# Maxima's rows on SP's queue 14 slots behind a block's input, four extra maxima rounds in output units, score heads together amid projections

## The chip, the cores and the metric

The kernel runs on one core of a Trainium2 chip. The metric is the device time of one execution in microseconds, the median of three runs: 2252.01 us (2251.91 to 2252.19). Five engines work side by side, each through its own queue in order: TensorE (PE; its weight loads are shown as PEld), VectorE (DVE), ScalarE (ACT), GpSimd (POOL) and SyncE (SP), which here only issues DMAs. DMAs are issued by SP and, a few, by ACT.

## The reference

One sequence of 2048 tokens with 576 features goes through attention with 32 heads of 18 features, and through an MLP with 4608 hidden features behind a layer norm; a gate for each token mixes the two.

```python
def reference(A_x, A_wqkv, A_wo, B_x, B_w1, B_b1, B_w2, B_b2, gate_w):
    x = A_x
    g = _sigmoid((x * gate_w).sum(-1, keepdims=True))
    a = _A_ref(x, A_wqkv, A_wo)          # softmax(q k^T / sqrt(18)) v, then wo
    b = _B_ref(x, B_w1, B_b1, B_w2, B_b2)  # gelu(layernorm(x) w1 + b1) w2 + b2
    return g * a + (1 - g) * b
```

## The kernel before, in words

Matmuls run in a rounded 32-bit format; where precision matters an operand is split into a high and a low part, and three products are summed. A first stage (to about 237 us) makes Q, K, V and the normed tokens and writes them to DRAM. Then comes one long loop, in which attention and MLP are woven into each other, and at the end the output projection.

**Attention.** A unit is a pair of heads and half of the queries; there are 32 units of 16 key blocks, so 512 steps. The softmax's maximum is taken in a first pass: `s1_round` (L216) computes for a query tile and 512 keys the scores of both heads (matmul L227, one head on rows 0 to 53 of the array, the other on rows 64 to 117), and VectorE reduces them (L229). A unit has 32 such rounds. When a unit's rounds are done, `s1_finish` (L232) turns the maxima into two rows for each head, which are stored into rows 54 and 55 of the unit's Q tile `qa` with eight small DMAs from the tile `mr` (L257, issued in helper line L134; these are "the rows" below), so that the second pass `s2` (L299) gets scores that are shifted by the maximum already: score matmul L310 on 56 rows, then the exponential on ScalarE (L312) into a ring of tiles. `pv` (L327) multiplies them with V (L338) for several steps at once.

In a step of the loop, `s2` runs twice: head 0's score, a round of a later unit between, head 1's score. Where there is no round, head 1's score (`tail`) is held back (`held`) until the next `flush()`, and other PE work stands between the two heads. Score tiles of the first pass rotate over three PSUM banks, those of the second over two.

**MLP.** Tokens come in 4 blocks of 512, hidden features in 9 groups of 4 chunks. For each group, `h_pair` (L554) computes two chunks of hidden features (matmul L581, input `Y`, weights W1), then a GELU chain on ACT, POOL and DVE; `out_pair` (L677) is the output unit: one tile of 128 tokens, 24 pairs of matmuls (L713, weights W2) in two turns, with a lent round between the turns (`lend_round`), and two sums on DVE (L687). The W2 tiles of a group are four (`w3` in the program, 4 buffers), so the next group's can be loaded only when the last output unit of this group has read them. In the first block they are split on ACT and POOL from raw weights (L475, L480); later they are reloaded from `w_scr` (one DMA of 576 KB each, L134). At a change of the token block, `load_y` (L738) loads the next block's input while the last `h_pair` of the old block still runs; its DMAs stand in SP's queue and wait for parts of the old input to be read.

**Order and queues.** All is written out by hand: generators yield pieces of MLP work, `fill` (L1339) puts them between a step's parts, and `run_due` counts slots; work put off with `defer(n, ...)` runs n slots later. The framework keeps each engine's order and adds the semaphores. Each DMA counts on one of eight completion semaphores, handed out in turn in the order in which the framework lists the instructions, and is issued only when the DMA before it on the same semaphore has landed. The rows go out on SP at once, in a bundle, unless `slot[0] < ybusy[0]`: then they go out on ScalarE's queue, one in each of the next eight slots. `load_y` sets `ybusy` to 30 slots ahead each time it is called, so that the rows don't stand on SP behind the input.

**Four rounds more.** The loop takes two rounds in each step. So that the rounds end earlier, four are taken ahead of the loop, and four more (`extra`, `LEAD = 4`) at the first four PV products of the loop (L1391), by `next_round`, a round with both heads in a row.

**The end.** When MLP work is used up (after about 2165 us), `fill` takes matmuls of the output projection (`out_proj`, L1300, on all 128 rows) to put between the scores, eight in each gap. Behind the last PV, the denominators of the last unit go through DRAM (L351 to L368) and are loaded for the last blocks (L1201); ACT and DVE prepare the blocks (L1227 to L1239), PE does what is left of the projections.

Of the kernel before, what the change touches and what calls it, by code (L numbers as in the profile page):

```python
# [29 lines left out]
G = 4  # L30
# [10 lines left out]
LEAD = 4  # L41
# [19 lines left out]
def gated_mix_kernel(ctx: ExitStack, tc: tile.TileContext, x, wqkv, wo, w1, b1, w2, b2, gate_w, out):  # L61
# [58 lines left out]
    def psum(pool):  # L120
        return pool.tile([P, TB], F32, name="ps")

    def big_tile():
        return yp.tile([P, 9, TB], F32R, name="big")
# [12 lines left out]
    slot = [0]  # L137
    later = []

    def defer(n, fn):  # L140
        later.append((slot[0] + n, fn))
# [128 lines left out]
    ybusy = [0]  # L270
# [4 lines left out]
    def flush():  # L275

        if held:
            for fn in waiting:
                fn()
            waiting.clear()  # L280
            tail = held.pop()
            tail()
# [94 lines left out]
    def take_round():  # L377
        u, r = rounds.pop()
        head = s1_round(u, r)
        if r == NR - 1:  # L380
            defer(1, lambda: s1_finish(u))
        return head

    def next_round():
        if rounds:
            flush()
            head = take_round()
            for h in range(2):
                head(h)


    lent = [0]

    def lend_round():
        if rounds and not lent[0]:
            next_round()
            lent[0] = 1
# [7 lines left out]
    def mlp():  # L405
# [90 lines left out]
        def ready(table, key):  # L496
            while key not in table:
                bg.pop(0)[1]()
            return table[key]
# [35 lines left out]
        def cuts(n, pieces):  # L535

            return {(k * n + pieces - 1) // pieces for k in range(1, pieces)}
# [3 lines left out]
        def free_pool():  # L541

            if rounds:
                return ps_w
            turns[0] += 1
            return (ps_s1, ps_w)[(turns[0] - 1) // 2 % 2]
# [130 lines left out]
        def out_pair(i, t, acc):  # L677

            tb, g = seq[i]
            tok = slice(t * P, (t + 1) * P)  # L680
            cs = [slice(nn * ND, (nn + 1) * ND) for nn in range(2)]
            bare = not rounds

            def add(ps, base):
                for nn in range(2):
                    dst = acc[:, t, cs[nn]]
                    nc.vector.scalar_tensor_tensor(dst, ps[nn][:, :ND], 0.5, b2b[:, cs[nn]] if base else dst,  # L687
                                                   op0=ALU.mult, op1=ALU.add)
            ps = [psum(free_pool()) for _ in range(2)]
            ends = {7, 15} if piece[0] == 0 else cuts(24, max(1, 3 - piece[0]))  # L690
            k = 0
            for turn in range(2):
                if turn == 1:
                    flush()
                if turn == 1 and bare:
                    add(ps, g == 0)
                    ps = [psum(free_pool()) for _ in range(2)]
                elif turn == 1:
                    if 3 * G not in ends:
                        lend_round()  # L700
                    turned[0] += 2
                    nc.tensor.wait_ge(turn_sem, turned[0])
                for j in ORDER:
                    while (i, j) not in HT:
                        cut[0] = 3
                        yield 0
                    hh, hl = HT[i, j]
                    w_ = ready(W2, (i * (G // 2) + j // 2, j % 2))
                    for h_, p_ in ((hh, 0), (hh, 1), (hl, 0)):
                        def head(h, h_=h_, p_=p_, w_=w_, k=k, turn=turn, ps=ps):  # L710
                            r = slice(64 * h, 64 * h + 64)
                            nn = h ^ turn
                            mm = nc.tensor.matmul(ps[nn][:, :ND], h_[r, tok], w_[p_][r, cs[nn]],  # L713
                                                  start=(k == 0 or bare and k == 3 * G), stop=(k == 6 * G - 1 or bare and k == 3 * G - 1))
                            if bare:
                                return
                            if k == 3 * G - 1:
                                mm.then_inc(turn_sem, 1)
                                tc.no_tile_sem_insts.add(mm.ins.name)
                                tc.add_to_no_dep_group(f"turn{turned[0]}", mm.ins)  # L720
                            elif k == 3 * G and h == 0:
                                tc.declare_fence(mm.ins, group=f"turn{turned[0] - 2}")
                        weave((0, 1) if turn == 0 else (1, 0), [partial(head, 0), partial(head, 1)], 2)
                        k += 1
                        if k < 6 * G:
                            if k in ends:
                                cut[0] = 1
                            yield 131
            flush()
            add(ps, g == 0 and not bare)  # L730
            if g == NG - 1:
                tt = TBS[tb] * 4 + t
                nc.gpsimd.tensor_scalar(acc[:, t, :], acc[:, t, :], gate1[:, tt:tt + 1], 1.0, op0=ALU.mult, op1=ALU.mult)
                defer(12 if tb < NB - 1 else 4, lambda: nc.sync.dma_start(b_scr[tt * P:(tt + 1) * P, :], acc[:, t, :]))
            cut[0] = 2
            yield 131

        def load_y(tb, s_, c0=0, c1=9):  # L738
            if s_ not in Y:
                Y[s_] = big_tile()  # L740
            ybusy[0] = slot[0] + 30
            for h in range(2):
                dma_r(nc.sync, Y[s_][64 * h:64 * h + 64, c0:c1, :], y_scr[TBS[tb], s_, c0 + h:c1 + h].rearrange("c p n -> p c n"))

# [84 lines left out]
    def filler(upto):  # L829

        while stream and spent[0] < upto:
            try:
                spent[0] += next(stream[0])
            except StopIteration:
                stream.pop(0)
            end, cut[0] = cut[0], 0
            if end == 3:
                break
        run_due()
# [499 lines left out]
    def fill(step):  # L1339

        t = spent[0]
        gap = gaps[0]
        gaps[0] += 1
        if over[0] is None and stream:
            behind[0] = base + (TOTAL - KEPT - base) * step / BARE
            ended[0] = atom() == 2
            piece[0] += 1
            run_due(max(spent[0] - t, GAP))
        if over[0] is None and not stream:
            stream.append(proj)  # L1350
            over[0] = gap - (spent[0] == t)
            spent[0] = 0.0
        if over[0] is not None and over[0] < gap:
            filler(PROJ * 122.5 * (gap - over[0]))
            run_due()

    looped[0] = True
    done = [0]
    due_v = []
    extra = [LEAD]  # L1360
    gaps = [0]
    for u in range(NU):
        for kc in range(NT):
            step = u * NT + kc
            if kc == 1:
                if u + 2 < NU:
                    load_q(u + 2)
                if u % 2 == 0 and u // 2 + 1 < NPAIR - 1:
                    load_k(u // 2 + 1)
                    due_v.append((u * NT, u // 2 + 1))  # L1370
                elif u == NU - 5:
                    ring_stack.close()
                    kp = ctx.enter_context(tc.tile_pool(name="c_ka", bufs=1, side="right"))
                    KA.append(kp.tile([P, S], F32R, name="ka2"))
                    for j in range(2):
                        nc.gpsimd.memset(KA[2][64 * j + 32:64 * j + 64, :].bitcast(F32), 1.0)
                    load_k(NPAIR - 1)
                elif u == NU - 4:
                    due_v.append((u * NT, NPAIR - 1))
            at[0] = step  # L1380

            room[0] = 3 if step < NARROW - 3 else 2
            while due_v and due_v[0][0] <= done[0]:
                load_v(due_v.pop(0)[1])
            s2(u, kc, 0, loop_round(), 462.0)
            if step - done[0] >= room[0] or room[0] == 3 and ended[0] and step > done[0]:
                pv(done[0], step)
                done[0] = step
                piece[0] = 0
                ended[0] = 0  # L1390
                if extra[0]:  # L1391
                    next_round()
                    extra[0] -= 1
            else:
                fill(step)
            s2(u, kc, 1, loop_round(), 462.0)
            if not (room[0] == 3 and ended[0]):
                fill(step)
# [29 lines left out]
```

## Time and profile before

| | |
|---|---|
| median of 3 runs | 2252.01 us |
| the profiled execution itself | 2253.85 us |
| its span in the profile | 2252.1 us |
| mean granted PE clock | 0.997 |
| chain that ended last, share of PE | 95% |
| first stage, loop, projections behind the last PV | to 237, to 2201, to 2249 us |

Times in the profile are microseconds from the start of the span. A row of the timeline gives the start and the length of a group of instructions, engine and line, output <- input, and in brackets the idle time just before it with what ended it. The chain of waits is followed back from the last instruction: what held the end at each moment. Releasers are inferred from semaphores. The granted clock is the share of full speed that PE was allowed. PE's matmuls are pipelined, so neighbours overlap in the timeline.

### The profile page before, as it was taken

Reading aid. Unit: us, or ns where it says so; the run is one execution under the profiler, and the core shown is the slowest. Engines: PE = TensorE matmul, PEld = TensorE weight load, DVE = VectorE, ACT = ScalarE, POOL = GpSimd, SP = SyncE. Lnnn points to the kernel's source line nnn. Section 1 sums busy time; section 2 is a strip of 40 time slices with the busy share of each in tenths; the row PEclk is TensorE's granted clock in tenths of the full one; section 3 lists DMA queues with packets and bytes.
Section 4 is the critical chain, followed back from the end, with each engine's and each line's share of the span. In section 5 each row is a group of like instructions: output and inputs, shape, how many; then the busy total and the mean of one; then the engine's idle time right before and its main releaser. Section 6 shows DMA issues by size and latency. Waiting matters only on the chain.

```text
span 2252.1 us, 51151 instructions
## 1 busy us (share of the span) xinstructions
PE 2228.8 (99%) x20569; PEld 1619.0 (72%) x20569; DVE 1651.6 (73%) x2887; ACT 1440.2 (64%) x2719; POOL 947.0 (42%) x936
## 2 busy tenths in 40 slices
PE   8999999999999999999989999999999999999999
PEld 7878677777677767767667677776676677777768
DVE  5675777777777777777767777777777777777734
ACT  4223677777766666666656666666766667666761
POOL 4002466666654444444435444444534444433420
PEclk9999999999999999999999999999999999999999
DMA  7765654546375434332363424233554333333255
GB/s 243 262 189 183 188 170 146 161 139 191 141 212 183 123 108 132 99 121 99 115 159 141 122 99 122 99 123 120 140 178 114 135 111 103 111 105 113 97 183 169
DMA packets 163411, 323.62 MB, mean 144 GB/s; under 512 B 59838, under 2 KB 86370, under 8 KB 152338
## 3 DMA queue, kind: packets, MB, share of 16 engines
q1 hardware_dynamic: 159174, 313.57, 43.9%
q10 hardware_dynamic: 4000, 6.78, 0.8%
q8 instruction: 162, 2.65, 0.5%
q14 instruction: 75, 0.61, 0.1%
HBM read 229.07 MB, written 95.16 MB: 144 GB/s over the span
## 4 chain that ended last, share of the span: by engine, by line
PE 95%; DVE 2%; DMA 2%; POOL 1%; ACT 1%; issue 0%; SPq 0%; ACTq 0%; DVEq 0%; POOLq 0%
PE ps L338 20%; PE ps L713 20%; PE ps L581 20%; PE ps L310 14%; PE ps L227 11%; PE ps L990 5%; PE ps L1008 2%; PE ps L1300 1%; PE ps L905 1%; DVE m L229 0%; PE ps L1039 0%; DMA x<-in_A_x_dram 0%; DMA w<-w_scr 0%; DMA qa<-mr 0%; DMA ot_scr<-dn_scr 0%
## 5 line engine op out<-in xcount | busy, mean ns | idle before, releaser
L229 DVE TENSOR_REDUCE m<-ps 128x1 f32<-128x512 f32 x2048 | 1302.3, 684 | 333.5 <-PE ps L227 306.5
L312 ACT ACTIVATE p<-ps 128x512 f32<-128x512 f32 x1080 | 587.0, 596 | 294.3 <-PE ps L227 198.9
L310 PE MATMUL ps<-qa,ka 56*128 56x512 f32 x2048 | 704.7, 411 | 3.2 <-DMA qa<-mr 2.1
L312 ACT ACTIVATE ring<-ps 128x512 f32<-128x512 f32 x968 | 525.8, 596 | 282.0 <-PE ps L227 210.4
L227 PE MATMUL ps<-ka,qa 54*128 54x512 f32 x2048 | 648.8, 416 | 3.3 <-DVE m L229 2.2
L713 PE MATMUL ps<-w,hh 64*128 64x288 f32 x4352 | 530.6, 297 | 1.0 <-ACT z L606 0.6
L581 PE MATMUL ps<-big,w 64*128 64x512 f32 x3888 | 516.9, 392 | 0.1
L310 PEld LDWEIGHTS ps<-qa,ka 56*128 56x128 f32 x2048 | 362.4, 185 | 212.0 <-issue 70.1
L180 POOL TENSOR_SCALAR zz<-zz 128x512 f32<-128x512 f32 x272 | 168.2, 619 | 760.5 <-ACT zz L669 728.1
L581 PEld LDWEIGHTS ps<-big,w 64*128 64x128 f32 x3888 | 378.1, 185 | 76.4 <-ACT vt L1019 0.3
L713 PEld LDWEIGHTS ps<-w,hh 64*128 64x128 f32 x4352 | 420.1, 186 | 15.0 <-ACT z L606 1.0
L180 POOL TENSOR_TENSOR zz<-zz,z 128x512 f32<-128x512 f32 x280 | 361.3, 1290 | 36.6 <-ACT zz L671 10.5
L227 PEld LDWEIGHTS ps<-ka,qa 54*128 54x128 f32 x2048 | 339.0, 186 | 36.0 <-DVE m L229 11.8
L713 PE MATMUL ps<-w,hl 64*128 64x288 f32 x2176 | 361.6, 292 | 0.0
L338 PE MATMUL ps<-p,vt 128*32 128x512 f32 x2160 | 265.2, 598 | 0.0
L713 PEld LDWEIGHTS ps<-w,hl 64*128 64x128 f32 x2176 | 247.8, 186 | 1.2
L338 PE MATMUL ps<-ring,vt 128*32 128x512 f32 x1936 | 238.3, 598 | 0.0
L180 POOL TENSOR_TENSOR w<-x,w 128x576 fp32r<-128x576 f32 (+1 forms) x34 | 68.3, 2012 | 276.9 <-ACT w L475 253.8
L180 POOL TENSOR_TENSOR hl<-zz,hh 128x512 fp32r<-128x512 f32 x134 | 174.2, 1300 | 14.5 <-ACT hh L632 3.7
L687 DVE SCALAR_TENSOR_TENSOR x<-ps,x 128x288 f32<-128x288 f32 x268 | 110.2, 453 | 86.9 <-PE ps L713 78.1
L338 PEld LDWEIGHTS ps<-p,vt 128*32 128x32 f32 x2160 | 57.9, 109 | 126.9 <-issue 125.7
L338 PEld LDWEIGHTS ps<-ring,vt 128*32 128x32 f32 x1936 | 52.1, 109 | 112.8 <-issue 112.8
(120 smaller groups left out, 1471.6 us busy)
## 6 DMA issues: line engine op xcount, KB each, us to landing
w<-w_scr SPq DMA_DIRECT2D x54, 1152.0 KB
w<-w_scr SPq DMA_DIRECT2D x108, 576.0 KB
w_scr<-w SPq DMA_DIRECT2D x18, 1152.0 KB
w_scr<-w SPq DMA_DIRECT2D x36, 576.0 KB
qa<-qk_scr SPq DMA_DIRECT2D x192, 72.0 KB
ka<-qk_scr SPq DMA_DIRECT2D x90, 144.0 KB
big<-y_scr SPq DMA_DIRECT2D x48, 256.0 KB
x<-in_B_w_dram SPq DMA_DIRECT2D x34, 288.0 KB
```

The lines of the kernel that those rows point to most:

```text
L180: fn(*args, **kw)
L227: nc.tensor.matmul(ps, qa[r0:r0 + 54, t * P:(t + 1) * P], ka[r0:r0 + 54, kb * TB:(kb + 1) * TB], start=True, stop=True)
L229: nc.vector.tensor_reduce(M4[u][:, h, t, kb:kb + 1], ps, axis=AX.X, op=ALU.max)
L310: nc.tensor.matmul(ps, ka[r0:r0 + 56, kc * P:(kc + 1) * P], qa[r0:r0 + 56, qb * TB:(qb + 1) * TB], start=True, stop=True)
L312: nc.scalar.activation(ring(n)[:, qb, h], ps, AF.Exp, scale=SCALE)
L338: nc.tensor.matmul(OB[u][r:r + 32, :], v[:, k, 19 * h:19 * h + 32], ring(c)[:, qb, h, :], start=(k == 0), stop=(k == NT - 1))
L581: nc.tensor.matmul(ps[h], wt[w_][r, c, :], Y[s_][r, c, :], start=(k == 0), stop=(k == 26))
L687: nc.vector.scalar_tensor_tensor(dst, ps[nn][:, :ND], 0.5, b2b[:, cs[nn]] if base else dst, op0=ALU.mult, op1=ALU.add)
L713: mm = nc.tensor.matmul(ps[nn][:, :ND], h_[r, tok], w_[p_][r, cs[nn]], start=(k == 0 or bare and k == 3 * G), stop=(k == 6 * G - 1 or bare ...
L905: nc.tensor.transpose(ps[:, t * P:(t + 1) * P], x_view(tb)[:, t, c * P:(c + 1) * P], ident)
L990: nc.tensor.matmul(ps, w_[:, c, ms], big[:, s_, :], start=(k == 0), stop=(k == len(prods) - 1))
L1008: nc.tensor.matmul(ps[:, :ND], big[:, s_, tok], w_[:, c, cs], start=(k == 0), stop=False)
```

## The change

Three edits. The rows go to ScalarE's queue only up to 14 slots behind a call of `load_y`, not 30. The four extra rounds aren't taken at the first PV products any more, but within the first four output units, in the second turn, when 20 of the 24 pairs are out. And when `fill` puts projections into a gap, the held score of head 1 is let out first.

```diff
@@ -390,6 +390,7 @@
 
     lent = [0]
+    extra = [LEAD]
 
     def lend_round():
...
@@ -722,6 +723,9 @@
                         weave((0, 1) if turn == 0 else (1, 0), [partial(head, 0), partial(head, 1)], 2)
                         k += 1
+                        if k == 5 * G and extra[0]:
+                            extra[0] -= 1
+                            next_round()
                         if k < 6 * G:
...
@@ -738,7 +742,7 @@
                 Y[s_] = big_tile()
-            ybusy[0] = slot[0] + 30
+            ybusy[0] = slot[0] + 14
...
@@ -1351,13 +1355,13 @@
         if over[0] is not None and over[0] < gap:
+            flush()
             filler(PROJ * 122.5 * (gap - over[0]))
             run_due()
...
-    extra = [LEAD]
     gaps = [0]
...
@@ -1388,9 +1392,6 @@
                 ended[0] = 0
-                if extra[0]:
-                    next_round()
-                    extra[0] -= 1
             else:
```

What moves is little, and each of it in one place. Of 32 units two had their rows on ACT, at the first and at the second change of the input block (about 671 and 1158 us). Around the second one SP's queue stood so before (`w3` are the four W2 reloads, `w4` a W1 reload, `big` the input `Y`):

```order
L134 DMA big_1868<-y_scr_66 64x2x512 x2
L134 DMA big_1306<-y_scr_66 64x2x512 x2
L368 DMA ot_scr_67<-dn_scr_68 36x1x1024
L134 DMA w3_16554<-w2_scr_65 128x1152
L134 DMA w3_16556<-w2_scr_65 128x1152
L134 DMA w3_16558<-w2_scr_65 128x1152
L134 DMA w3_16560<-w2_scr_65 128x1152
L134 DMA w4_16732<-w1_scr_64 128x2304
L353 DMA dn_16840<-oe_16839 128x1x16
```

and ACT's, with the rows between the exponentials (L312):

```order
L134 DMA qa0_109<-mr_16626 2x8x32 x2
L312 ACTIVATE p_2674<-ps_16653 128x512
L312 ACTIVATE p_2674<-ps_16662 128x512
L134 DMA qa0_109<-mr_16626 2x8x32
L606 ACTIVATE z_16676<-ps_16562,b1t_77 128x512
L134 DMA qa0_109<-mr_16626 2x8x32
L312 ACTIVATE ring2_2271<-ps_16687 128x512
L312 ACTIVATE ring2_2271<-ps_16696 128x512
L134 DMA qa0_109<-mr_16626 2x8x32
```

Now ACT has none of them, and SP has all eight between the four W2 reloads and the W1 reload:

```order
L134 DMA w3_16554<-w2_scr_65 128x1152
L134 DMA w3_16556<-w2_scr_65 128x1152
L134 DMA w3_16558<-w2_scr_65 128x1152
L134 DMA w3_16560<-w2_scr_65 128x1152
L134 DMA qa0_109<-mr_16626 2x8x32 x8
L134 DMA w4_16733<-w1_scr_64 128x2304
L353 DMA dn_16840<-oe_16839 128x1x16
```

In the framework's list of all engines, the rows on ACT stood ahead of the W2 reloads on SP and were given their semaphores first; now they come behind them. Around the first change the eight rows stand on SP behind the last input load and ahead of the four stores L480.

The extra rounds, on PE, at the end of one of the first output units (the last L713 here belong to the next unit), before:

```order
L310 MATMUL ps<-qa_109,ka_112 128x512
L227 MATMUL ps<-ka_112,qa_110 128x512 x2
L310 MATMUL ps<-qa_109,ka_112 128x512
L338 MATMUL ps<-ring_2271,vt_114 32x512 x4
L338 MATMUL ps<-ring_2279,vt_114 32x512 x4
L227 MATMUL ps<-ka_112,qa_110 128x512 x2
L310 MATMUL ps<-qa_109,ka_112 128x512
L227 MATMUL ps<-ka_112,qa_110 128x512 x2
L310 MATMUL ps<-qa_109,ka_112 128x512
L713 MATMUL ps<-w_2054,hh 128x288 x4
```

and now, from within the unit:

```order
L714 MATMUL ps<-w_2101,hh 128x288 x4
L227 MATMUL ps<-ka_112,qa_110 128x512 x2
L714 MATMUL ps<-w_2101,hl 128x288 x2
L714 MATMUL ps<-w_2082,hh 128x288 x4
L714 MATMUL ps<-w_2082,hl 128x288 x2
L310 MATMUL ps<-qa_109,ka_112 128x512
L227 MATMUL ps<-ka_112,qa_110 128x512 x2
L310 MATMUL ps<-qa_109,ka_112 128x512
L338 MATMUL ps<-ring_2271,vt_114 32x512 x4
L338 MATMUL ps<-ring_2279,vt_114 32x512 x4
L310 MATMUL ps<-qa_109,ka_112 128x512
L227 MATMUL ps<-ka_112,qa_110 128x512 x2
```

The extra round stood directly ahead of the loop's round; between the two are now eight output matmuls, a round and the PV products. This is so in four units. On DVE the two reductions of the round come ahead of the unit's sums L687.

The scores amid projections, on PE from the first L1300 on, before:

```order
L310 MATMUL ps<-qa_110,ka_28066 128x512 x2
L1300 MATMUL ps<-big 128x288 x8
L310 MATMUL ps<-qa_110,ka_28066 128x512
L1300 MATMUL ps<-big 128x288
L310 MATMUL ps<-qa_110,ka_28066 128x512
L1300 MATMUL ps<-big 128x288
L1300 MATMUL ps<-wlast,big 128x288
L1300 MATMUL ps<-big 128x288 x2
```

and now (L1300 is L1304 there):

```order
L310 MATMUL ps<-qa_110,ka_28066 128x512 x2
L1304 MATMUL ps<-big 128x288 x8
L310 MATMUL ps<-qa_110,ka_28066 128x512 x2
L1304 MATMUL ps<-big 128x288 x2
L1304 MATMUL ps<-wlast,big 128x288
L1304 MATMUL ps<-big 128x288 x2
```

One or two projection matmuls stood between the heads at eight places up to the last PV products; now none do. On ACT the exponential of head 1 moves ahead of some of the block preparations (L1230) that `filler` lets run.

## The prediction

> **What bounds the kernel now.** I read the page's table of engines first, then the list of what TensorE waited for.
>
> ```profile
> PE 2228.8 (99%) x20569; PEld 1619.0 (72%) x20569; DVE 1651.6 (73%) x2887; ACT 1440.2 (64%) x2719; POOL 947.0 (42%) x936
> ```
>
> TensorE (PE) is busy for 2228.8 of 2252.1 us, and no other engine is above three quarters. The instructions on PE are the same in both kernels, 18523 of them in either order, so a gain can come only from the 23.3 us in which PE stands, from time in which it runs at a lower clock, or from neighbours in its queue that overlap better. The list of PE's waits names what stands (engine, line, releaser: us in total, times, longest):
>
> ```profile
> PE ps L713 <- DMA w<-w_scr: 6.1, 2, 5.8
> PE ps L227 <- DVE m L229: 2.2, 4, 0.5
> ```
>
> The first row is, but for 0.3 us, one stall in the middle of the program; the second is four short ones near its start. (PE also waits for the first load, which the change doesn't touch.) I then read the timeline of the stall, PE first (start, us, instructions, in brackets the idle time before them and its releaser), and for comparison the same stretch one group of the MLP earlier.
>
> ```profile
> 1135.06 1.92 PE L338 MATMUL ps<-p,vt 128*32 128x512 f32 x16
> 1143.20 1.06 PE L338 MATMUL ps<-ring,vt 128*32 128x512 f32 x8
> ...
> 1161.64 1.07 PE L338 MATMUL ps<-ring,vt 128*32 128x512 f32 x8
> 1164.93 0.43 PE L713 MATMUL ps<-w,hh 64*128 64x288 f32 x4
> ...
> 1172.26 0.60 PE L713 MATMUL ps<-w,w 64*128 64x288 f32 x2 [5.80 <-DMA w<-w_scr]
> 1178.52 1.92 PE L338 MATMUL ps<-ring,vt 128*32 128x512 f32 x16
> ```
>
> From the start of three steps of PV products, over an output unit, to the next PV products PE takes 1143.20 - 1135.06 = 8.14 us in a normal group, and 1178.52 - 1161.64 = 16.88 us here. So this place costs **8.74 us**, although the wait itself is 5.80. The windows (length, busy time of PE, PEld, DVE, ACT and POOL, granted PE clock, DMA share, GB/s) show the rest:
>
> ```profile
> 1150.00:1160.00 10.00, 10.00 (x88) 6.91 (x86) 7.78 (x16) 5.85 (x13) 0.00 (x0) 1.00 0.03 10
> 1170.00:1175.00 5.00, 2.74 (x18) 2.46 (x20) 1.29 (x2) 1.60 (x3) 0.00 (x0) 0.55 0.47 190
> 1175.00:1180.00 5.00, 5.00 (x48) 3.56 (x46) 3.14 (x6) 2.69 (x5) 0.92 (x2) 0.77 0.00 0
> ```
>
> After the stall the granted clock is 0.55 and then 0.77; the 2.9 us beyond the wait are lost there. The page "TensorE: Matmul & The Clock Gate" of the Trainium skill (section "The HAM clock gate") says that an idle window of about 3.4 us halves PE's clock until it has been busy for about as long. An estimate from that page is 1.7 us lost behind the stall and a sum smaller by 1.2 us; the trace has 2.9, and the measurement decides. The first window is as telling: from 1150 to 1160 the DMA engines are busy for a share of 0.03. The weights come late because they are asked for late. The timelines of SP and ACT (SPq and ACTq rows are DMA issues) and SP's waits say why:
>
> ```profile
> 1143.73 0.64 SPq L368 DMA_DIRECT2D ot_scr<-dn_scr  x1
> 1160.39 6.28 SPq L134 DMA_DIRECT2D w<-w_scr  x5
> ...
> 1158.60 0.64 ACTq L134 DMA_DIRECT2D qa<-mr  x1
> 1165.83 0.62 ACTq L134 DMA_DIRECT2D qa<-mr  x1
> ...
> SPq L134 <- DMA qa<-mr: 20.3, 4, 16.0
> ```
>
> SP issues nothing for 16 us, and what it waits for is the rows of maxima on ScalarE's queue. Each DMA counts on one of eight semaphores, handed out in turn, and has to wait for the DMA before it on the same one. The rows, spread over slots on ACT, were given theirs just ahead of the four reloads of W2, so each reload waits for one row: the first reload starts 1.8 us after the first row was issued.
>
> **Place 1: the rows go to SP (at the first and the second change of the input block).** With 14 slots in the place of 30 two units' rows change queue, 16 issues in all. At 1158 us they now stand behind the four reloads of W2 on SP, so the reloads wait only for PE to have read the old W2, which is the end of the output unit before: the same order as at the third block change, where the trace shows it at work without any PE wait:
>
> ```profile
> 1615.82 20.83 SPq L134 DMA_DIRECT2D big<-y_scr  x20
> 1638.58 3.66 SPq L134 DMA_DIRECT2D w<-w_scr  x4
> 1654.82 5.30 SPq L134 DMA_DIRECT2D qa<-mr  x8
> ```
>
> PE's next PV products after that unit are these (chain of waits):
>
> ```profile
> 1150.57 1.85 PE ps L338 x16
> ```
>
> So the reloads can go out just before, from 1150, and PE wants the first at 1164.93. In the old run the four went out from 1160.39 and had landed by 1172.26, under 12 us; they fit into the 15. The rows are ready by 1158.60, take 5.30 us to issue as in the row above, so to 1164, and are needed by the next unit's scores behind the PV products that then come at 1178.52 - 8.74 = 1169.8. The one W1 reload behind them on SP leaves at about 1164, no later than now (it is the fifth of the row at 1160.39, which ends at 1166.67). I take the whole **8.7 us**. Late next would be the rows, 5 us behind; the bounds are 8.74 and, if the reloads still come late, 0. The page "DMA: Bandwidth & Descriptors" of the Trainium skill (section "Issuing engines are not separate DMA queues") speaks against the move: transfers of all issuing engines share the same DMA engines, and another queue saves only the time of the issue. By that rule alone this place would give nothing and the sum would be 5.7 us. The trace doesn't bear it out: DMA stood idle before the stall (0.03), so it was order that was short and not bandwidth.
>
> At the first block change (671 us) there is no stall, but the projection beside the rows is slow. Chain of waits, and ACT's timeline:
>
> ```profile
> 672.46 0.43 PE ps L310
> 682.45 2.71 PE ps L338 x24
> ...
> 1125.84 0.43 PE ps L310
> 1135.13 2.71 PE ps L338 x24
> ...
> 671.42 1.95 ACTq L134 DMA_DIRECT2D qa<-mr  x2
> ```
>
> 682.45 - 672.46 = 9.99 us against 9.29 for the same projection in a normal group, because two issues held ACT for 1.95 us and the exponentials, then the score banks, came late. SP is free there. I take the difference, **0.7 us** (bounds 0 and 0.7).
>
> **Place 2: the four extra rounds.** Before, an extra round stands behind the PV products, directly ahead of the loop's own, and there the three PSUM banks run out. Timeline of PE:
>
> ```profile
> 277.59 0.73 PE L227 MATMUL ps<-ka,qa 54*128 54x512 f32 x3
> 278.88 0.49 PE L227 MATMUL ps<-ka,qa 54*128 54x512 f32 x1 [0.55 <-DVE m L229]
> 279.21 0.44 PE L713 MATMUL ps<-w,hh 64*128 64x288 f32 x4
> ...
> 1145.06 0.73 PE L227 MATMUL ps<-ka,qa 54*128 54x512 f32 x2
> 1145.63 0.43 PE L713 MATMUL ps<-w,hh 64*128 64x288 f32 x4
> ...
> 1140.63 0.35 PE ps L227 x2
> ...
> 269.78 4.97 DVE L229 TENSOR_REDUCE m<-ps 128x1 f32<-128x512 f32 x8 [0.72 <-PE ps L227]
> ```
>
> With the extra round it is 279.21 - 277.59 = 1.62 us from the end of PV to the output unit, without it 0.57. So a round costs 1.05 there, 0.55 of it the wait. Inside an output unit a round takes 0.35 (a lent round, from the chain). Between the lent round and the moved one PE has 16 output matmuls, and behind it 8 more, a round and then PV, which uses none of these banks. VectorE needs 4.97 / 4 = 1.24 us for a round's two reductions, ran eight in a row there before, and now gets them spread; so the banks should come free in time. 4 x (1.05 - 0.35) = **2.8 us**; if a new wait of 0.55 takes the place of the old one, 4 x 0.15 = 0.6. I take 2.5, near the upper end.
>
> **Place 3: the tail.** While the last projections fill the gaps, the second head's score matmul now stands directly behind the first at eight places. Chain, both forms side by side in the run of before:
>
> ```profile
> 2166.70 0.42 PE ps L310 x2
> 2167.13 1.25 PE ps L1300 x8
> 2168.38 0.43 PE ps L310
> 2168.81 0.33 PE ps L1300
> 2169.13 0.42 PE ps L310
> 2169.56 1.13 PE ps L1300 x7
> ```
>
> Together: 0.42 + 1.25 = 1.67 us; apart: 0.43 + 0.33 + 0.42 + 1.13 = 2.31. Two neighbouring heads take as long as one alone (0.42 and 0.43): they stand in different rows of the array and overlap. 8 x 0.64 = 5.1 us at most. Not all of that arrives. In the last stretch, which holds three of the eight, ACT is already nearly full:
>
> ```profile
> 2189.50:2201.20 11.70, 11.05 (x65) 5.46 (x64) 8.31 (x15) 8.38 (x16) 0.00 (x0) 1.00 0.91 323
> ```
>
> Taking 3 x 0.64 and PE's idle time there (11.70 - 11.05 = 0.65) away leaves 9.1 us with 8.38 of ACT work and an output DMA to issue, in a fixed order, and the DMA share is 0.91, so loads of the next blocks can't come much earlier either. Behind the last PV stands a chain of transfers (denominators out, back, and into the last projections); if it moves less than PE, PE waits for it. I take half, **2.5 us**, with the ends 5.7 (all, and the old wait with it) and -1 (the small transfers queue behind a block load on SP).
>
> **The sum.** 8.7 + 0.7 + 2.5 + 2.5 = 14.4 us. The profiled execution took 2253.85 us around its span of 2252.1, 1.84 above the median of 2252.01; I take the sum off both: a span of 2237.7 and a median of 2237.6 us.
>
> **The rivals.** (a) The stall at 1166 stays in part, because the reloads of W2 wait for something else than the rows: with all of it left the gain is 5.7 us, 2246.3. For it speaks that the last reload alone took from 1165.9 to 1172.26; against it that DMA stood idle from 1150 to 1160 and that the third change has the new order without a stall. That the change doesn't do what it says is this rival's worst form. Chance 0.10. The rule of the Trainium skill on issuing engines, above, would end here. (b) The tail gives back what it gains, because the last unit's chain doesn't move: 2252.0 - 11.9 = 2240.1. Chance 0.15. (c) Slower: the rows on SP fall behind block inputs that still wait for their buffers, and the next unit's scores wait for the rows. An input's issues take up to 20.83 us (row above); rows behind a whole input would come that much later, less the 5 us that they have to spare, so PE would stand 15 us at both places, with 2.9 more for the clock: 2 x 18 us against 5 gained elsewhere, 2283. It decides only where the last input issue is later than the rows; here it ends 15 us ahead at the second change (1143.7 against 1158.6). Chance 0.02.
>
> **How the numbers follow.** Forecast 0.73, 2237.6, by its own bounds from 2234 to 2241. The range takes in rival (b) and half of (a): **2233.8 to 2243.5**, with about 0.12 above or below. A measurement of this kernel tells about 0.2% from no change, 4.5 us. Below 2247.5 lie the forecast, (b) and nearly all of (a): faster 0.94, same 0.04, slower 0.02.
>
> **What would show it.** Right: no PE wait on w<-w_scr over 0.5 us and a granted clock of 1.00 through the middle; the W2 reloads issued near 1150 and the rows behind them on SP; no wait of L227 on L229 near 260 to 290 us; score matmuls in pairs amid L1300, and the last PV products ending 2 to 5 us less than now behind the first L1300 (2201.2 - 2167.13 = 34.1 us). Wrong: a PE wait on qa<-mr after a block change, an equal wait on w, or PE waits on ACT and DVE in the tail that add up to more than 3 us.

## The result and the profile after

| | before | after |
|---|---|---|
| median (lowest to highest), six runs each, side by side | 2252.1 (2250.61 to 2258.29) us | 2239.03 (2237.59 to 2240.08) us |
| ratio after / before, 95% interval | | 0.9937 [0.9924, 0.995] |
| span of the profiled execution | 2252.1 us | 2238.3 us |

The change makes the kernel 13 us faster in medians, 13.8 in the two profiled spans. The page's row of engines after, then two rows of the list of what PE waited for (L713 is now L714, L1300 L1304, L1309 L1313):

```profile
PE 2222.0 (99%) x20569; PEld 1619.8 (72%) x20569; DVE 1651.7 (74%) x2887; ACT 1440.2 (64%) x2719; POOL 949.1 (42%) x936
```

```profile
PE ps L310 <- DMA qa<-mr: 2.6, 2, 1.8
PE ps L1304 <- DVE res L1313: 1.0, 1, 1.0
```

Neither the wait for w<-w_scr nor the four for m L229 are in the list any more. The largest wait left inside the loop is the 2.6 us for the first unit's rows near 250 us, which is in both kernels (2.1 before).

**The second change of the input block.** SP's timeline, then the windows of the same stretch (columns as in the prediction):

```profile
1143.02 0.64 SPq L368 DMA_DIRECT2D ot_scr<-dn_scr  x1
1147.86 2.99 SPq L134 DMA_DIRECT2D w<-w_scr  x4
1157.29 5.31 SPq L134 DMA_DIRECT2D qa<-mr  x8
1162.70 0.34 SPq L134 DMA_DIRECT2D w<-w_scr  x1
```

```profile
1150.00:1160.00 10.00, 10.00 (x88) 7.14 (x82) 7.90 (x16) 6.29 (x15) 0.00 (x0) 1.00 0.59 217
...
1170.00:1175.00 5.00, 5.00 (x61) 4.08 (x53) 4.67 (x9) 2.54 (x5) 4.66 (x7) 1.00 0.17 41
```

The four reloads leave SP at 1147.86, 12.5 us earlier than at 1160.39, and the DMA engines, idle here before (a share of 0.03), are now busy for 0.59. PE is busy without a gap at a granted clock of 1.00.

**The extra rounds.** PE's timeline, the first five PV products of the loop; the first two rows are before, the other five after:

```profile
258.67 1.92 PE L338 MATMUL ps<-p,vt 128*32 128x512 f32 x16
...
296.33 1.92 PE L338 MATMUL ps<-p,vt 128*32 128x512 f32 x16
```

```profile
261.14 1.92 PE L338 MATMUL ps<-p,vt 128*32 128x512 f32 x16
...
269.45 1.92 PE L338 MATMUL ps<-ring,vt 128*32 128x512 f32 x16
...
277.22 1.92 PE L338 MATMUL ps<-p,vt 128*32 128x512 f32 x16
...
284.99 1.92 PE L338 MATMUL ps<-ring,vt 128*32 128x512 f32 x16
...
296.18 1.92 PE L338 MATMUL ps<-p,vt 128*32 128x512 f32 x16
```

From the first to the fifth it takes 296.18 - 261.14 = 35.04 us, and took 296.33 - 258.67 = 37.66.

**The tail.** PE's timeline, the first matmuls of the output projection and the start of the last PV products, before and after:

```profile
2167.06 1.32 PE L1300 MATMUL ps<-big 128*128 128x288 f32 x8
...
2199.35 1.06 PE L338 MATMUL ps<-p,vt 128*32 128x512 f32 x8
```

```profile
2157.43 1.32 PE L1304 MATMUL ps<-big 128*128 128x288 f32 x8
2158.68 0.50 PE L310 MATMUL ps<-qa,ka 56*128 56x512 f32 x2
...
2184.76 1.06 PE L338 MATMUL ps<-p,vt 128*32 128x512 f32 x8
```

2199.35 - 2167.06 = 32.29 us became 27.33. These rows cut the span into stretches, which shows where the time went:

| stretch | before | after | difference |
|---|---|---|---|
| start to the first PV of the loop | 258.67 | 261.14 | +2.47 |
| to the fifth PV (the extra rounds) | 37.66 | 35.04 | -2.62 |
| to the first projection matmul (both block changes) | 1870.73 | 1861.25 | -9.48 |
| to the last PV (the pairs) | 32.29 | 27.33 | -4.96 |
| to the end of the span | 52.75 | 53.54 | +0.79 |
| sum | 2252.10 | 2238.30 | -13.80 |

Two stretches became longer. Whether the change does that, and whether the three gains stand by themselves, is asked of the runs.

### The profile page after: what moved, and what is told of

Same layout as the page of the kernel before. It is cut to its first block, busy times and chain, and to the rows that moved or that the text cites. A ratio compares the mean times of both kernels' runs of the same rounds, so it can differ in the third digit from the quotient of the medians.

```text
span 2238.3 us, 51156 instructions
## 1 busy us (share of the span) xinstructions
PE 2222.0 (99%) x20569; PEld 1619.8 (72%) x20569; DVE 1651.7 (74%) x2887; ACT 1440.2 (64%) x2719; POOL 949.1 (42%) x936
## 4 chain that ended last, share of the span: by engine, by line
PE 96%; DVE 1%; DMA 1%; POOL 1%; ACT 1%; SPq 0%; issue 0%; ACTq 0%; DVEq 0%; POOLq 0%
PE ps L338 21%; PE ps L714 20%; PE ps L582 20%; PE ps L310 14%; PE ps L227 11%; PE ps L994 5%; PE ps L1012 2%; PE ps L1304 2%; PE ps L909 1%; PE ps L1043 0%; DMA x<-in_A_x_dram 0%; DVE m L229 0%; POOL zz L180 0%; DMA ot_scr<-dn_scr 0%; DMA dn_scr<-dn 0%
## 5 line engine op out<-in xcount | busy, mean ns | idle before, releaser
L229 DVE TENSOR_REDUCE m<-ps 128x1 f32<-128x512 f32 x2048 | 1302.7, 684 | 327.1 <-PE ps L227 273.5
L312 ACT ACTIVATE p<-ps 128x512 f32<-128x512 f32 x1080 | 586.7, 596 | 290.7 <-PE ps L227 185.4
L310 PE MATMUL ps<-qa,ka 56*128 56x512 f32 x2048 | 701.0, 411 | 3.2 <-DMA qa<-mr 2.6
L312 ACT ACTIVATE ring<-ps 128x512 f32<-128x512 f32 x968 | 525.8, 596 | 270.9 <-PE ps L227 175.9
L227 PE MATMUL ps<-ka,qa 54*128 54x512 f32 x2048 | 648.5, 415 | 1.2 <-DVE big L925 0.8
L714 PE MATMUL ps<-w,hh 64*128 64x288 f32 x4352 | 530.3, 296 | 0.7 <-ACT z L607 0.6
L310 PEld LDWEIGHTS ps<-qa,ka 56*128 56x128 f32 x2048 | 360.8, 185 | 213.3 <-issue 75.0
L714 PEld LDWEIGHTS ps<-w,hh 64*128 64x128 f32 x4352 | 421.1, 186 | 14.2 <-ACT z L607 1.0
L714 PE MATMUL ps<-w,hl 64*128 64x288 f32 x2176 | 363.5, 292 | 0.0
L227 PEld LDWEIGHTS ps<-ka,qa 54*128 54x128 f32 x2048 | 339.4, 185 | 29.3 <-DVE m L229 5.7
L714 PEld LDWEIGHTS ps<-w,hl 64*128 64x128 f32 x2176 | 248.4, 185 | 1.1
```

Source lines behind the costliest of these rows:

```text
L227: nc.tensor.matmul(ps, qa[r0:r0 + 54, t * P:(t + 1) * P], ka[r0:r0 + 54, kb * TB:(kb + 1) * TB], start=True, stop=True)
L229: nc.vector.tensor_reduce(M4[u][:, h, t, kb:kb + 1], ps, axis=AX.X, op=ALU.max)
L310: nc.tensor.matmul(ps, ka[r0:r0 + 56, kc * P:(kc + 1) * P], qa[r0:r0 + 56, qb * TB:(qb + 1) * TB], start=True, stop=True)
L312: nc.scalar.activation(ring(n)[:, qb, h], ps, AF.Exp, scale=SCALE)
```

## The experiments

The theory: the stall came from reloads that shared completion semaphores with rows issued late; the extra rounds ran out of PSUM banks only because two rounds stood next to each other; the pairs overlap at all eight places; the three add up. Rivals stand with each run.

### Each part alone

Three kernels are the kernel before with one edit of the change each. The rows:

```diff
-            ybusy[0] = slot[0] + 30
+            ybusy[0] = slot[0] + 14
```

> The kernel before with 14 in the place of 30 slots and nothing else. Theory (the stall was made by the order of the completion semaphores, and the three parts add up): the second block change gives 8.8 us and the first 0.65, as between the two profiles, so about 2252.1 - 9.4 = 2242.7; no PE wait on w<-w_scr above 0.5 us, the waits of L227 on L229 still there at 260 to 290 us, the tail as before (last PV products 2199 less 9.4). Rival (the parts lean on each other, say because VectorE or the banks are fuller without the other two): less than 8 us, with the lost part as a PE wait after 1145 us.

The extra rounds alone (the first and the last pieces of the diff, nothing else):

> The kernel before with the four extra rounds inside the output units and nothing else. Theory: the stall at 1166 to 1172 stays with its 5.8 us, the four waits of L227 on L229 go, and the first five PV products stand 2.3 us closer together: about 2249.8. Rival (the 2.1 us by which the changed kernel's first PV came later are made by the moved rounds, and not by chance): the first PV product starts near 261.1 instead of 258.7 us and the time stays at 2252. If the start differs by chance, it may lie anywhere from 258.5 to 261.5 in this run too, so the distance from the first PV product to the fifth decides: 35.0 us by the theory (37.7 before).

The pairs alone:

```diff
         if over[0] is not None and over[0] < gap:
+            flush()
             filler(PROJ * 122.5 * (gap - over[0]))
```

> The kernel before with the score heads of the tail together and nothing else. Theory (the pairs overlap at all eight places and ScalarE keeps up): the last PV products come 4.9 us earlier behind the first matmul of the last projections (34.1 us before, 27.3 less the 2.1 that the start of the row may differ in the changed kernel), some 0.8 us of it are lost to a wait at the end, so 4.2 us: 2247.9. Rival of the prediction (half of it arrives, 2.5 us): 2249.6. Rival (the tail gives all back to the chain of transfers): 2252.1 with a PE wait of several us behind the last PV.

| | median us | ratio to before [95%] | gain by the ratio, us |
|---|---|---|---|
| rows alone | 2245.17 | 0.9965 [0.9952, 0.9979] | 7.9 (4.7 to 10.8) |
| rounds alone | 2251.33 | 0.9994 [0.9985, 1.0002] | 1.4 (-0.5 to 3.4) |
| pairs alone | 2248.62 | 0.998 [0.9971, 0.999] | 4.5 (2.3 to 6.5) |
| all three | 2239.03 | 0.9937 [0.9924, 0.995] | 14.2 (11.3 to 17.1) |

The expected medians were 2242.7, 2249.8 and 2247.9 us; all three came out higher, by 2.5, 1.5 and 0.7, while the kernel before stood at 2252.6 beside them. 7.9 + 1.4 + 4.5 = 13.8 against 14.2: within these wide intervals the parts add up. The traces say more sharply that none leans on another, since each stretch is as long with its part alone as with all three. With the rows alone no wait on w<-w_scr is left, and the PV products on both sides of its place start at 1162.94 and 1170.22 us, 7.28 apart (7.26 in the changed kernel). With the pairs alone PE's timeline has

```profile
2164.50 1.32 PE L1300 MATMUL ps<-big 128*128 128x288 f32 x8
...
2191.82 1.07 PE L338 MATMUL ps<-p,vt 128*32 128x512 f32 x8
```

which is 27.32 us as in the changed kernel, and its span ends 2243.9 - 2191.82 = 52.08 us behind that PV: no more than before (52.75). The wait at the end that the theory expected isn't there, so the rivals that give back half or all of it fall by this trace (the medians alone exclude only the one that gives back all: half, 2.5 us, lies inside 2.3 to 6.5). With the rounds alone:

```profile
259.93 1.92 PE L338 MATMUL ps<-p,vt 128*32 128x512 f32 x16
...
294.97 1.92 PE L338 MATMUL ps<-p,vt 128*32 128x512 f32 x16
```

35.04 us again, to the last digit, though the medians of whole runs hardly tell this gain from nothing.

The two kernels without the row edit hold something that none expected: the stall is smaller there. PE's waits with the rounds alone and with the pairs alone (6.1 us in the kernel before):

```profile
PE ps L714 <- DMA w<-w_scr: 4.0, 2, 3.4
```

```profile
PE ps L713 <- DMA w<-w_scr: 4.2, 1, 4.2
```

And the PV products on both sides of it, in PE's timeline of the kernel before, with the rounds alone, with the pairs alone, and after:

```profile
1162.53 1.90 PE L338 MATMUL ps<-p,vt 128*32 128x512 f32 x16
...
1178.52 1.92 PE L338 MATMUL ps<-ring,vt 128*32 128x512 f32 x16
```

```profile
1161.16 1.90 PE L338 MATMUL ps<-p,vt 128*32 128x512 f32 x16
...
1174.11 1.92 PE L338 MATMUL ps<-ring,vt 128*32 128x512 f32 x16
```

```profile
1162.62 1.90 PE L338 MATMUL ps<-p,vt 128*32 128x512 f32 x16
...
1176.02 1.92 PE L338 MATMUL ps<-ring,vt 128*32 128x512 f32 x16
```

```profile
1161.68 1.90 PE L338 MATMUL ps<-p,vt 128*32 128x512 f32 x16
...
1168.94 1.92 PE L338 MATMUL ps<-ring,vt 128*32 128x512 f32 x16
```

Without a stall this takes 7.26 us, with it 15.99, 12.95 and 13.40: the same stall cost 8.73, 5.69 and 6.14 us in three executions. The rows alone gain 7.9 in medians, between these with the 0.65 of the first block change on top.

### Queue or semaphore

In the changed kernel, half of the rows of the two units go back to ScalarE's queue. Those four get semaphores that the W2 reloads don't take:

```diff
-            aside = slot[0] < ybusy[0]
+            aside = u in (7, 15)
...
-                if aside:
-                    defer(1 + n, lambda n=n: store(*divmod(n, 4)))
+                if aside and n < 4:
+                    defer(1 + n, lambda n=n: store(*divmod(n, 4), nc.scalar))
                 else:
                     store(*divmod(n, 4))
```

> The changed kernel with the rows of the units at the two changes of the input block split: four of eight still on ScalarE's queue, spread over slots, the other four at once on SP. The semaphores of the four that stay on ScalarE's queue are then not those of the W2 reloads behind them, which take the ones of older, landed DMAs and of the rows on SP. Theory (it is the sharing of semaphores that made the stall): the reloads go out from about 1148 to 1157, no PE wait on w<-w_scr above 0.5 us, time within 1 us of the changed kernel's 2239.0, although rows still leave on ScalarE's queue up to 1162. Rival (a row on ScalarE's queue as such, by its issue or by what it keeps ScalarE from, made the stall): the wait stays, 2.5 to 5.8 us, and the time is 2243 to 2248.

2241.06 us, ratio 0.9944 [0.9929, 0.9959], and no PE wait on w<-w_scr. I had expected a time within 1 us of 2239.0; it is 2.1 above (the intervals of the two ratios overlap). SP's timeline, and ACT's:

```profile
1148.71 3.42 SPq L134 DMA_DIRECT2D w<-w_scr  x4
1159.64 3.42 SPq L134 DMA_DIRECT2D qa<-mr  x4
```

```profile
1157.85 0.64 ACTq L134 DMA_DIRECT2D qa<-mr  x1
...
1160.62 0.62 ACTq L134 DMA_DIRECT2D qa<-mr  x1
```

Rows leave on ScalarE's queue from 1157.85 to 1160.62, and the reloads have been out since 1148.71. So ScalarE's queue did not make the stall; the semaphores did. (In the program the four rows on ScalarE's queue stand ahead of the reloads here too, but the reloads have the semaphores of older input loads; the four rows on SP stand behind them. At the first block change the four rows still cost ScalarE time: from the PV products that start at 670.51 us to those at 681.76 it takes 11.25 us, against 10.31 in the changed kernel: 0.9 of the 2.1 us.)

Then the other way round: all eight rows on ScalarE's queue, one behind the other:

```diff
-                if aside:
-                    defer(1 + n, lambda n=n: store(*divmod(n, 4)))
-                else:
-                    store(*divmod(n, 4))
+                store(*divmod(n, 4))
```

(with `aside` as above.)

> The changed kernel with all eight rows of the two units at the changes of the input block on ScalarE's queue again, but issued one directly behind the other as on SP, not spread over slots. The W2 reloads then take the semaphores of four of these rows again. Theory (semaphores shared with the rows): the first reload leaves SP only after the first row has landed, near 1160 us, though the rows are issued without gaps; a PE wait on w<-w_scr of 3 to 6 us comes back, and a stretch of half clock behind it; from the PV products at 1160.8 to the next PV 13 to 16 us in the place of 7.3. Rival (it was the spreading over slots that made the reloads late, not the semaphores): the eight rows are out within 5.3 us, the last three reloads follow sooner than in the kernel before, and the wait falls below 2 us.

One execution: 2253.94 us, 15 above the changed kernel. PE's waits, and the second block change in the timelines of ACT, SP and PE (L307, L309 are L310, L312 here):

```profile
PE ps L307 <- ACT p L309: 10.2, 2, 5.6
```

```profile
1164.47 5.41 ACTq L134 DMA_DIRECT2D qa<-mr  x8
```

```profile
1166.30 8.03 SPq L134 DMA_DIRECT2D w<-w_scr  x5
```

```profile
1170.57 0.52 PE L307 MATMUL ps<-qa,ka 56*128 56x512 f32 x1 [4.61 <-ACT p L309]
```

The first reload leaves 1.83 us behind the first row (1.79 in the kernel before), and SP's wait for it is 15.8 us, so it does wait for that row's landing. But my expectation named the wrong wait: none on w<-w_scr comes back. ScalarE issues the eight rows for 5.41 us and computes no exponential meanwhile, PE runs out of scores at both block changes, and the reloads come behind that in time. From PV products to PV products the first change takes 18.80 us (669.86 to 688.66; 10.31 in the changed kernel) and the second 16.87 (1157.72 to 1174.59; 10.27), which is the 15 us. Spread over slots, as in the kernel before, the same eight cost PE no such wait; on SP they need no spreading.

### The first block change

```diff
-            ybusy[0] = slot[0] + 14
+            ybusy[0] = slot[0] + 20
```

> The changed kernel with 20 in the place of 14 slots: the rows at the first change of the block (17 slots behind the input) go back to ScalarE's queue, those at the second (25 slots) stay on SP. Theory: only the first change differs, and from the PV products there to those behind the projection it takes 10.97 us as in the kernel before (10.31 in the changed one); the second change runs without a wait; the time is 0.65 us above the changed kernel's, less than one run tells. Rival (the queue's state at the first change has a part in the stall at the second): a wait on w<-w_scr near 1165.

One execution: 2237.94 us, too near the changed kernel's to tell 0.65. The trace tells it: from the PV products that start at 669.25 us to those at 680.23 it takes 10.98 us; in the changed kernel from 671.13 to 681.44, 10.31. There is no wait at the second change. The two places have nothing to do with each other, and the first gives 0.67.

### How near two rounds may stand

```diff
-                        if k == 5 * G and extra[0]:
+                        if k == 4 * G and extra[0]:
```

> The changed kernel with the four moved rounds eight output matmuls earlier, so eight behind the lent round in the place of 16. Theory (a round stalls when VectorE has not yet emptied the three banks of the round before): eight output matmuls of 0.13 us are 1.1 us, less than the 1.24 us that two reductions take, so waits of L227 on L229 of a few tenths each come back, 0.5 to 2 us over the four, and the first five PV products lie 35.5 to 37 us apart (35.04 in the changed kernel). Rival (any place inside the output unit is good, since the wait before came from the round directly ahead alone): no such wait and 35.0 us.

The expectation was wrong: one execution took 2238.33 us, and PE's timeline has

```profile
260.17 1.92 PE L338 MATMUL ps<-p,vt 128*32 128x512 f32 x16
...
295.05 1.93 PE L338 MATMUL ps<-p,vt 128*32 128x512 f32 x16
```

34.88 us, without any wait of L227. Eight output matmuls between two rounds are enough. I had asked for both reductions to be done, but there are three banks and a round takes two, so as I read it a round needs only one of the two banks of the round before. The four waits came from two rounds directly one behind the other.

### The first unit's rows

The wait for the first unit's rows near 250 us looks like the stall again: rows asked for late. So they were asked for earlier in the changed kernel, by 4 and by 5 slots:

```diff
-            defer(2 if looped[0] else 8, rows)
+            defer(2 if looped[0] else 4, rows)
```

> The changed kernel with the rows of the first unit four slots earlier (4 in the place of 8). It aims at what is left of the changed kernel's start: PE waits 2.6 us for the rows of the first unit at 249 to 253 us and runs at half clock for 6.8 us there, which is 3.4 us of work lost. Theory (the rows are late because they are asked for late, as the reloads were): the wait goes or falls below 1 us, and with it the half clock in part, 2 to 5 us less than the changed kernel, 2234 to 2237. Rival (the rows wait for their maxima and not for their place in the order): the wait stays at 2.6 us and the time at 2239.

It was 2236.45 us, 0.9926 [0.9912, 0.9939]. Since that stood beside the kernel before and not beside the changed one, all three were then run side by side:

> The changed kernel once more, so that it stands on the same chip beside the versions with earlier rows. 2239.0 within 1 us. If the place of the half clock near 250 us and the length of the row's start differ by chance, the first PV product starts anywhere from 259 to 261.5 us, and what follows it keeps its distances: 35.0 us over the first five PV products, 27.3 from the first matmul of the last projections to the last PV.

> The version with 4 in the place of 8 slots once more, beside the changed kernel on one chip. Theory (it takes the 2.6 us wait for the first unit's rows away): 2 to 3 us below the changed kernel in the same call. Rival (the 2.6 us between the two medians were the difference of two chips): within 1 us of it.

> The changed kernel with 3 in the place of 8 slots. Theory: with 4 slots the wait for the rows had gone already and what PE waits for there is ScalarE and VectorE, so the same as with 4 slots within 1 us. Rival (still earlier rows also take the rest of the half clock away): another 1.7 us. Rival (the rows now wait on SP for their maxima and hold the W2 and block transfers behind them): slower than with 4 slots by 1 us or more.

| slots | median us (lowest to highest) | ratio to before [95%] |
|---|---|---|
| 8 (the changed kernel) | 2239.0 (2237.91 to 2240.22) | 0.9936 [0.9923, 0.995] |
| 4 | 2236.11 (2235.6 to 2237.07) | 0.9923 [0.9911, 0.9936] |
| 3 | 2235.61 (2235.16 to 2236.26) | 0.9921 [0.9908, 0.9935] |

The runs of 4 and of 3 slots all lie below all of the changed kernel: 2.9 and 3.4 us. In their lists of PE's waits the one for qa<-mr is gone with 4 slots and 0.2 us with 3. Windows of the changed kernel and of the one with 4 slots:

```profile
250.00:255.00 5.00, 2.78 (x13) 1.83 (x15) 2.53 (x5) 2.80 (x6) 3.41 (x3) 0.68 0.23 75
255.00:260.00 5.00, 5.00 (x43) 4.48 (x42) 3.47 (x7) 3.83 (x8) 1.28 (x1) 0.64 0.67 175
```

```profile
250.00:255.00 5.00, 4.31 (x27) 3.32 (x26) 4.03 (x7) 4.73 (x9) 3.51 (x4) 0.66 0.54 161
255.00:260.00 5.00, 4.89 (x50) 2.76 (x48) 4.09 (x8) 3.75 (x8) 0.94 (x2) 1.00 0.96 159
```

PE is busy for 4.31 in the place of 2.78 us. These two are faster than both kernels of this change; 3 and 4 slots can't be told apart.

## Why the prediction was right, and where its terms were off

The forecast of 2237.6 us is 1.4 below the median, inside the forecast's own bounds of 2234 to 2241.

- **Place 1, second block change (8.7).** The mechanism is as told: the reloads leave early, DMA fills the idle window, PE goes through at full clock, and the rows, 9.4 us behind the reloads, are in time. Rival (a), a stall that stays, is ruled out by the changed kernel itself, and half_act's split shows which of two things it was, queue or semaphore, which the prediction had only argued. The Trainium skill, page "DMA: Bandwidth & Descriptors", section "Issuing engines are not separate DMA queues", says that another queue gives no bandwidth; its rule alone would have left the stall, and the run shows why it doesn't bear here: what the move changed was the order of waiting, not the queue. The size is that of one execution: 8.73, 5.69 and 6.14 us in three. I took the largest without saying that a stall's price can differ from one execution to the next. Of the 2.9 us beyond the wait that the prediction put down to the clock, 0.31 is the shorter of PE's two waits on w<-w_scr, at 1165.80.
- **Place 1, first block change (0.7).** 0.65 between the two profiles, 0.67 with the rows put back.
- **Place 2 (2.5).** 2.62 from the first to the fifth PV, of which 0.35 only went ahead of the first PV with the round that now stands in the first output unit: 2.27. No new wait took the old one's place.
- **Place 3 (2.5).** This term was mis-sized: 4.96 us, of 5.1 at most, came from the eight pairs. I had halved it because ScalarE was nearly full in the last stretch and a chain of transfers stands behind the last PV. ScalarE kept up but for two pairs of 0.86 and 0.81 us in the place of 0.50. Behind the last PV the stretch to the end is 52.08 to 53.77 us in ten executions with the pairs (in the middle 53.06) and 52.07 to 52.81 in three without (52.75). PE's wait on DVE res in that stretch is up to 1.0 us with the pairs and up to 0.4 without. So a few tenths are given back by the middle values, 0.79 in the two profiles compared here, and not all that was gained: rival (b) is ruled out.
- **Not in the sum.** The start to the first PV: 2.47 us later. Programs that are the same up to there differ by chance: 258.67, 258.62 and 259.72 with the rounds at their old place (before, pairs alone, rows alone), 261.14, 260.30, 260.25, 259.93, 259.71 and 259.24 with a round in the first output unit. The moved round is 0.35 of the difference; of the other 1.1 between the middle values of the two groups I can't say whether it is chance. If it isn't, place 2 is worth about 1.2 us and not 2.27; the rounds alone gained 1.4 (-0.5 to 3.4).
- **A count.** The prediction's 18523 instructions on PE stand in no row. The page counts 20569 on PE in both kernels, and what the prediction drew from it, that they are the same, holds.

In the pair of profiles the 4.96 - 2.5 = 2.5 us that the tail gave beyond its term stand against 2.47 and 0.79 in the two stretches that grew, so that the sum fits so closely is in part luck. Rival (c), rows behind an input that still waits for its buffers, didn't come: the last input issue is out before 1143.02, the rows come at 1157.29.

## What to carry to other kernels

When a load comes late while the DMA engines are idle, look at what its issue waited for, and at which transfer had the same completion semaphore before: an unrelated small store on another queue can hold a large load. Spread a store over slots only on an engine that has other work to do, and never ahead of a load that something waits for. A stall read from one profile is one draw of its price, so take its range from several executions; and a gain that is counted place by place, each place with its own row, need not be halved because another engine is nearly full there: ScalarE's 8.38 us of work in 9.1 still fitted.

## What the hardware showed that I had not expected

A small store landed late while large loads were under way. In the kernel before, SP's four waits for rows are 16.0, 0.3, 2.8 and 1.2 us: the third reload leaves at 1164.3, though the third row, whose semaphore it shares, was issued at 1160.21. With the first two reloads under way that row took up to 4.1 us to land, where the first, on idle DMA engines, took at most 1.8. So the rows held two later reloads once more, and the last of the four left 5.5 us behind the first.

The reloads themselves took different times. Behind the long wait PE starts again at 1172.26 in the kernel before, and with the rounds alone and the pairs alone at

```profile
1168.74 0.61 PE L714 MATMUL ps<-w,w 64*128 64x288 f32 x2 [3.44 <-DMA w<-w_scr]
```

```profile
1170.48 0.56 PE L713 MATMUL ps<-w,w 64*128 64x288 f32 x2 [4.18 <-DMA w<-w_scr]
```

From the first reload's issue (1160.39, 1159.08, 1160.47) that is 11.87, 9.66 and 10.01 us, with the same transfers; the fourth reload leaves 5.3 to 5.5 us behind the first in all three. Over the ten us behind the first issue the DMA engines moved 278, 285 and 287 GB/s, each at a share of 0.84. Why the last of the four took longer in one of them, no run here tells; it is most of what made one wait 5.8 us and another 3.4.

Half clock comes in pieces of one length. In the kernel before the granted clock is 0.50 in each whole microsecond from 1171 to 1177 and 1.00 on both sides of that stretch, so the windows can be turned into time at half speed: 0.55 and 0.77 over 5 us each are 2 x (0.45 + 0.23) x 5 = 6.8 us. With the rounds alone:

```profile
1165.00:1170.00 5.00, 1.56 (x13) 1.22 (x11) 0.18 (x1) 0.22 (x1) 1.30 (x2) 0.84 0.93 338
1170.00:1175.00 5.00, 5.00 (x54) 4.00 (x54) 3.66 (x7) 3.83 (x8) 0.34 (x1) 0.82 0.18 76
```

2 x (0.16 + 0.18) x 5 = 3.4 us. Near 250 us it is 2 x (0.32 + 0.36) x 5 = 6.8 in the changed kernel and 2 x 0.34 x 5 = 3.4 with 4 slots. Of the thirteen traces nine have 6.8 to 6.9 there and four 3.4, none anything between, and the wait for the rows doesn't decide which: with the same wait of 2.6 us the runs of the changed kernel have 6.8 and slot20 3.4, and with 3 slots, where PE's longest wait there is 0.6 us, it is 6.9. So it is one piece or two, and this makes up the rest of the spread of the stall's price: 8.73 us for waits of 6.1 and two pieces, of which about 1.8 us passed while PE still waited; 5.69 for 4.0 and one; 6.14 for 4.2 and one. The page "TensorE: Matmul & The Clock Gate" of the Trainium skill (section "The HAM clock gate") has a window of 3.4 us that runs on whatever the kernel does. The pieces here have that length, but the prediction's estimate took one such window, which is half of the time at half clock that the kernel before had.
